# State products and levels of later units in one run on TensorE, outputs and new states laid out by head parity

## The chip, the cores and the metric

One core of one Trainium2 chip runs the whole program in one launch. The metric is the device time in microseconds (us) of one execution; the kernel before has a median of 587.53 us over three runs. Engines are named as in the profile: PE is TensorE (PEld its weight loads), DVE is VectorE, ACT is ScalarE, POOL is GpSimd, SP is SyncE, which issues most transfers.

## The reference

A linear-attention recurrence over 768 steps for 4 batches and 8 heads of width 48 is followed by a two-layer block with `h - tanh(h)` between its matrices, on 3072 tokens:

```python
state = zeros(B, H, D, D)                        # B, H, S, D = 4, 8, 768, 48
for t in range(S):
    cur = einsum('bhd,bhe->bhde', u * k[t], v[t])
    y[t] = einsum('bhd,bhde->bhe', r[t], state + cur)
    state = w * state + einsum('bhd,bhe->bhde', k[t], v[t])
x = y.transpose(0, 2, 1, 3).reshape(B * S, H * D)  # 3072 x 384
h = x @ w_in                                       # 384 -> 2048
out = (h - tanh(h)) @ w_out                        # 2048 -> 384
```

## The kernel before

The recurrence is done in chunks of 64 steps. A *unit* is one chunk (`ch`) of two batches (`z` = 0, 1); there are 24 units, two to a *block* `j` of the dense part, which has 12 blocks. Heads go in pairs: pair `p` = 0 to 3, head parity `i` = 0, 1. Even heads lie in rows 0 to 63, odd heads in rows 64 to 127 (`HEAD[i]`, of which 48 are data); the batch halves of 64 steps lie in `HALF[z]`. TensorE is used in 64x64 tiles for all of this: an operand's row half gives the tile's row, the output's row half its column.

A unit does, in this order:

- `turn`, or for later units `spread_out` and `across`: r and k are turned so that the head width lies across the partitions; scaled by powers of the decay, they become `rT` and `kT`.
- `from_state` (16 products): the state times `rT`, into `y_ps`. It opens the sum over what the unit's outputs will be.
- `levels` (16 products): `kT` times `rT` into `lev`. `V.copy_predicated` (`x.cp`) puts its upper triangle into the tile `at`, whose diagonal ScalarE has written (`diagonal`, L858).
- `outputs`: `v` times `at` is added in `y_ps`; then `to_state`: `kw` times `v` gives what is new in the state, in `kv_ps`.
- `to_xt` and `to_rest` copy `y_ps` on ScalarE, through `given`, to the dense part's operand `xt` and to `rest`. POOL then issues six transfers a block (`fill`, L945), which bring `rest` into the padding rows of `xt`.
- `keep` (L951; for the first two units ScalarE, L954) adds `kv_ps` to the state; `x.decay` (L1002) multiplies it by the decay.

Each product is one call of `put` (L760), and the profile has two matmul instructions for each, so 16 products show as x32. `y_ps` and `kv_ps` are the two halves of the two banks of `yk_ps`. The first dimension of a bank's data is the bank, which is `z` for `y_ps` and `kv_ps` and `i` for `lev`. For units from 2 on (`swap`), the output of parity `i` and batch `z` goes to rows `i ^ z` (`to`), and `given` swaps the odd batch back with two half-row copies.

The first 12 units (*early* ones; `two` is false) have `lev` in banks of their own (`x_banks`), and run `from_state` and `levels` together. The later twelve (`two`) have it in `yk_ps` next to `y_ps`, in the columns where `kv_ps` comes afterwards. For them `from_state` is a step by itself; then a copy of two numbers on ScalarE (`between`, to the tile `seen`, L886) must be done before `levels` may start. `levels` then adds without clearing (`start=not two`).

The dense part goes tile by tile: `h` (L171, TensorE), five passes on ScalarE (L180 to L188), four on VectorE (L195 to L201), then the second matrix, either plainly (`o`, L209) or with seven products for eight (`products`, L260, with sums on POOL at L245 to L249). The first six blocks go through it in passes of 4, 4 and 8 of its 16 column groups (`PASSES`), so that early tiles need only the weights that are converted first: the weights come as 64-bit floats and are converted on VectorE and ScalarE (L139 to L145).

The order on each engine is written out by a planner at build time. Every step is given to it by `add` with an engine, a cost in us, what it comes after, and for TensorE a count of instructions (`steps`). It looks for good due times by random search with a fixed seed, first for a simpler plan, then for the one that is used, which follows the simpler one for the first 90 us of planned time. A change of steps or costs so gives a new order everywhere.

Of the kernel before, what the change touches and what calls it, by code (L numbers as in the profile page):

```python
# [32 lines left out]
PAD = 64  # L33
AHEAD = 2
L = 2
FIRST = 6
# [267 lines left out]
class Plan:  # L304
# [9 lines left out]
    CHUNK, CHUNK_0, ASKED, COMES, FIRST = 256, 192, 55, 3.4, 9.5  # L314
# [233 lines left out]
def near(ctx, tc, r, k, v, w, u, out, shared, moe_w_in, moe_w_out):  # L548
# [3 lines left out]
    V, A, T, G, Q = nc.vector, nc.scalar, nc.tensor, nc.gpsimd, nc.sync  # L552
    d = shared["dims"]
    H, D, NP, NK, B, HEAD = d.H, d.D, d.NP, d.NK, d.B, d.HEAD
# [11 lines left out]
    def fixed(name, shape, dt=F32):  # L566
        return const.tile(shape, dt, name=name, tag=name)
# [9 lines left out]
    HALF = [slice(z * SHORT, (z + 1) * SHORT) for z in range(2)]  # L577
# [2 lines left out]
    rows = fixed("rows", [2 * NP, 2, PAD])  # L580
    V.memset(rows, 1.0)
    same = fixed("same", [128, SHORT])
    seen = fixed("seen", [1, 2])
    V.tensor_tensor(same, ident[:, :SHORT], ident[:, SHORT:], ALU.add)
    by, plus = (work.tile([128, NP, SHORT + 1], F32, name=x, tag=like) for x, like in (("by", "tg"), ("plus", "q")))
    V.memset(by[:, :, 0:1], 0.0)
# [14 lines left out]
    extra = [work.tile([128, 2, NK, PAD], F32, name=f"extra{i}", tag="s") for i in range(L)]  # L601
# [51 lines left out]
    y_ps = yk_ps[:, :, :256].rearrange("e z (p t) -> e z p t", p=NP)  # L653
    kv_ps = yk_ps[:, :, 256 : 256 + NP * D].rearrange("d z (p e) -> d z p e", p=NP)
# [39 lines left out]
    def lay_out(early, across_by):  # L694
# [3 lines left out]
        def add(*args, **more):  # L698
            return plan.add(*args, **more)

        now = [add(e, 1.25 if e == "ACT" else .87, lambda e=e, at=at, x=x: e_of[e].dma_start(out=rows[at : at + NP, :, :D], in_=x.rearrange("(p i) d -> p i d", i=2)), due=-1, data=.05)
               for e, at, x in (("SP", 0, w), ("ACT", NP, u))]
# [3 lines left out]
        now = add("DVE", .45, lambda: V.tensor_scalar(  # L706
            by[:, :, 1:], wcol[:, :, None].to_broadcast([128, NP, SHORT]), W_LOW, W_HIGH, ALU.max, ALU.min), [cols])
        now = add("DVE", .7, lambda: V.tensor_tensor_scan(
            power.rearrange(flat), by.rearrange(flat), plus.rearrange(flat), 0.0, ALU.mult, ALU.add), [now])

        ups = add("ACT", .6, lambda: None, [now])
        now = add("DVE", 1.75, lambda: V.reciprocal(inverse, power), [now])
        inverted = now
        doubled = add("ACT", .6, lambda: A.copy(twice, inverse[:, :, None, 1:].to_broadcast([128, NP, 2, SHORT])), [now])
        now = tabled = add("PE", .7, table, [doubled], steps=8)
# [3 lines left out]
        now = add("POOL", 1.0, bounds, [keeps])  # L719
        now = add("PE", .2, lambda: T.matmul(tab[0:1, 0:1], ok[:, 0, :1], shared["one"], start=True, stop=True), [now, downs])  # L720
        flagged = add("DVE", .15, lambda: V.tensor_scalar(shared["flag"], tab[0:1, 0:1], 128 * NP - 0.5, None, ALU.is_lt), [now])
        bonus = add("SP", .65, lambda: Q.dma_start(
            out=ub.rearrange("p h d -> p (h d)"),
# [17 lines left out]
        for n in range(weights.count):  # L741
# [8 lines left out]
            now = of + ([converted[n - 2]] if n >= 2 else [])  # L750
            for name, cost in (("DVE", .47), ("DVE", .47), ("ACT", .84), ("ACT", .84), ("DVE", .87), ("DVE", .87), ("DVE", .87)):
                now = [add(name, cost, step, now)]
# [6 lines left out]
        def put(*args, **how):  # L759
            T.matmul(*args, skip_group_check=True, **how)  # L760

        units, filled, last_h = [], {}, {}

        def unit(n):
# [5 lines left out]
            ch, half = divmod(n, 2)  # L770
            j, slot = divmod(n, L)
            steps_at = slice(ch * SHORT, (ch + 1) * SHORT)
            t = SimpleNamespace(at=ats[n % 2])
            rt, vt, kw, state = rts[n % (AHEAD + 1)], vts[n % (AHEAD + 1)], kws[n % 2], states[half]
            two = n >= early
# [6 lines left out]
            b1, b2, b3 = (units[n - i] if n >= i else none for i in (1, 2, 3))  # L782
            x = SimpleNamespace(rest=None, rk=None, du=None, own=None)
# [4 lines left out]
            swap = n >= SWAP  # L788
# [67 lines left out]
            def diagonal(hs):  # L856
                for h in hs:
                    A.mul(t.at[:, h % 2, h // 2], same, t.du[:, h : h + 1])  # L858
# [12 lines left out]
            def to(i, z):  # L871


                i = i ^ z if swap else i
                return slice(i * PAD, (i + 1) * PAD)

            def from_state():
                for p in range(NP if ch else 0):
                    for z in range(2):
                        for i in range(2):  # L880
                            put(y_ps[to(i, z), z, p], state[HEAD[i], z, p], t.rT[HEAD[i], p, z],
                                start=p == 0, stop=False)

            def between():

                A.copy(seen, y_ps[:1, :, 0, 0])  # L886

            def levels():
                if not two:
                    from_state()  # L890
                for p in range(NP):
                    for z in range(2):
                        for i in range(2):
                            put(lev[HALF[z], i, p], t.kT[HEAD[i], p, z], t.rT[HEAD[i], p, z], start=not two, stop=True)
# [5 lines left out]
            def outputs():  # L900
                for p in range(NP - direct):
                    for i in range(2):
                        for z in range(2):
                            put(y_ps[to(i, z), z, p], vt[HALF[z], 2 * p + i], t.at[HALF[z], i, p],
                                start=p == 0 and not ch, stop=p == NP - 1)
                for p in range(NK if direct else 0):
                    for i in range(2):
                        for z in range(2):
                            put(y_ps[to(i, z), z, p], extra[slot][HALF[z], i, p], t.at[HALF[z], i, NK],
                                start=False, stop=p == NK - 1)  # L910
                if not direct:
                    to_state()

            def to_state():
                for p in range(NP if more else 0):
                    for i in range(2):
                        for z in range(2):
                            put(kv_ps[i * PAD : (i + 1) * PAD, z, p], kw[HALF[z], 2 * p + i], vt[HALF[z], 2 * p + i, :D],
                                start=p == 0 or not two, stop=True)

            def given(out, y):

                def copy(out, y):
                    A.copy(out, y) if sign > 0 else A.activation(out, y, AF.Copy, scale=sign)  # L924

                if not swap:
                    copy(out, y)
                    return
                copy(out[:, 0], y[:, 0])
                for i in range(2):  # L930
                    copy(out[i * PAD : (i + 1) * PAD, 1], y[to(i, 1), 1])

            def to_xt():
                if slot == 0:
# [3 lines left out]
            def to_rest():  # L938
                if slot == 0:
                    filled[j] = work.tile([128, L, 2, SHORT], F32, name="rest", tag="rest")  # L940
                given(filled[j][:, slot], y_ps[:, :, NK])
# [26 lines left out]
            both = [x.turn, x.turn_k]  # L968
# [8 lines left out]
            if product:  # L977
                now = add("ACT", 1.05, own_k, [x.kT, w_us])
                x.own = add("PE", .7, own_levels, [now, x.rT, b2.out], steps=64)
                x.diag = add("DVE", .64, lambda: V.copy_predicated(t.at, same.bitcast(I32)[:, None, None, :].to_broadcast([128, 2, NP, SHORT]), own_lev), [x.own, b2.out])  # L980
            else:
                x.rk = add(*own_at, own, [x.r, x.k, b2.du, b1.rk if not b1.own else None])
                now = add(*own_at, lambda: V_or_G.tensor_tensor(t.rk, t.rk, ub, ALU.mult), [x.rk, bonus])
                x.du = add("DVE", .47, own_sum, [now, b2.diag])
                now = add("ACT", 1.0, lambda: diagonal(range(0, H // 2)), [x.du, b2.out])
                x.diag = add("ACT", 1.0, lambda: diagonal(range(H // 2, H)), [now])
            begun = []
            if two:
                now = add("PE", .68, from_state, both + [x.rT, b1.xt, b1.rest, b1.add, b2.decay, x.kT], steps=64)
                begun = [add("ACT", .15, between, [now])]  # L990
            x.lev = add("PE", .7 if two else (1.35 if swap else 1.75) if ch else .7, levels,
                        begun + [x.kT, x.rT, b2.out] + ([b2.decay, b1.xt, b1.rest, b1.add] if ch else []), steps=128 if ch and not two else 64)
            x.cp = add("DVE", .64, lambda: V.copy_predicated(t.at, before, lev), [x.lev, b2.out] + ([] if product else [x.diag]))  # L993
            x.out = now = add("PE", .95 if direct else 1.3, outputs,
                              [x.cp, x.diag, x.v, b1.xt, b1.rest, b1.add] + ([x.extra] if direct else [x.kw]), steps=96 if direct else 128)
            if direct:
                now = x.out = add("PE", .6, to_state, [now, x.kw], steps=64)
            x.xt = add("ACT", .96 if swap else .4, to_xt, [now, last_h.get(j - FIRST - 2) if slot == 0 else None])
            if not direct:
                x.rest = add("ACT", .62 if swap else .26, to_rest, [x.xt] + (filled.get((j - 2, "all"), []) if slot == 0 else []))  # L1000
            x.add = add("DVE" if ch else "ACT", .47 if ch else 1.2, keep, [x.out, x.rest, x.xt]) if more else None
            x.decay = x.add if not ch else add(*own_at, lambda: V_or_G.tensor_tensor(state[:, :, :, :D], state[:, :, :, :D], w_all, ALU.mult), [x.add]) if more else None  # L1002
            if direct:
# [95 lines left out]
        for n in range(early):  # L1099
            unit(n)  # L1100
        mixing()
        now, done = 22.0, 0
# [7 lines left out]
        for n in range(early, d.NU):  # L1110
            unit(n)
# [260 lines left out]
def kernel(  # L1372
# [29 lines left out]
    with tc.manual_schedule():  # L1402
        near(tc, r, k, v, w, u, out, shared, moe_w_in, moe_w_out)
# [39 lines left out]
```

## Time and profile before

| what | value |
|---|---|
| median of 3 runs (lowest to highest) | 587.53 us (587.31 to 587.86) |
| span of the profiled execution, first to last instruction | 585.9 us |
| mean granted TensorE clock | 0.999 |
| busy: PE, DVE, ACT, POOL | 570.1, 493.5, 395.6, 206.1 us |
| `h` matmuls, L171 | 281.0 us, 1152 instructions |
| seven products, L260 | 104.1 + 71.5 + 34.8 + 34.7 us |
| small products, L760 on `yk_ps` and `x_ps` | 15 to 16 us for each large group |

The profile shows one execution. For it the span stands, without the launch around it; the runs' median is 1.6 us above it. Busy times are unions of an engine's instructions. Starts of matmuls are measured and their ends are modelled, so the time that a piece of TensorE's work takes is best read from start to start. A row of the timeline merges instructions of one kind that follow each other: start, length, engine, line, operation, output and inputs, shapes, count, and in brackets the idle time before it with what ended it. A row of waits says who waited for whom, for how long in all, and how often.

### The profile page before, as it was taken

To read this page: it belongs to the slowest core of one execution; us is meant where nothing else is said; L and a number is where in the kernel's file an instruction comes from. 1 tells how busy PE (TensorE), PEld (TensorE's weight loads), DVE (VectorE), ACT (ScalarE), POOL (GpSimd) and SP (SyncE) were. 2 spreads that over 40 slices of the span, in tenths; PEclk is the share of its full clock that TensorE was granted. 3 is DMA by queue.
4 is the path that set the end of the run, shared out by engine and by line. 5 is a ranking of instruction groups with operands and counts; after the bars stand their busy time and mean duration, and the time that the engine had idled before them with its cause. 6 is when DMAs were issued, how large, how long until landed. Compare 5 with 4: busy or idle time off the path is not lost.

```text
span 585.9 us, 14391 instructions
## 1 busy us (share of the span) xinstructions
PE 570.1 (97%) x5493; PEld 481.6 (82%) x5493; DVE 493.5 (84%) x817; ACT 395.6 (68%) x893; POOL 206.1 (35%) x366
## 2 busy tenths in 40 slices
PE   8888999999999999999999999999999999999996
PEld 4566677677777699899889898989999899899995
DVE  5799969999999999977988999888877777646665
ACT  2698889979775585555575785775766765665552
POOL 6002212200000245355455465443534446354420
PEclk9999999999999999999999999999999999999999
DMA  6976986743200121232335432531223300100101
GB/s 123 216 146 123 172 201 122 159 107 80 84 0 1 20 49 28 39 56 45 52 55 90 89 57 41 96 45 32 42 43 48 57 3 8 29 8 1 27 2 31
DMA packets 138549, 38.49 MB, mean 66 GB/s; under 512 B 130760, under 2 KB 132904, under 8 KB 138472
## 3 DMA queue, kind: packets, MB, share of 16 engines
q1 hardware_dynamic: 133308, 30.30, 28.4%
q0 software_dynamic: 4992, 6.99, 5.3%
q8 instruction: 45, 0.74, 0.5%
q14 instruction: 32, 0.26, 0.2%
q10 hardware_dynamic: 172, 0.20, 0.1%
HBM read 31.66 MB, written 4.72 MB: 62 GB/s over the span
## 4 chain that ended last, share of the span: by engine, by line
PE 81%; DVE 9%; ACT 4%; issue 2%; DMA 2%; SPq 1%; POOL 0%; DVEq 0%; ACTq 0%; POOLq 0%
PE h L171 38%; PE p L260 27%; PE o L209 7%; PE yk_ps L760 6%; ACT at L858 1%; SPq L798 1%; DMA xt<-rest 1%; DVE g L201 1%; DVE tg L199 1%; PE h L688 1%; DVE g L195 1%; DVE power L144 1%; DVE at L993 1%; DMA first_k<-in_k_dram 1%; DVE tg L197 1%
## 5 line engine op out<-in xcount | busy, mean ns | idle before, releaser
L171 PE MATMUL h<-xt,w_in_sb 128*128 128x256 f32 x1152 | 281.0, 381 | 1.3 <-DVE w_in_sb L145 0.9
L171 PEld LDWEIGHTS h<-xt,w_in_sb 128*128 128x128 f32 x1152 | 213.1, 190 | 32.6 <-PE x_ps L810 1.1
L245 POOL TENSOR_TENSOR sg<-g 128x256 f32<-128x256 f32 x69 | 54.0, 783 | 224.7 <-DVE g L201 213.9
L260 PE MATMUL p<-mixed,sg 128*128 128x192 f32 x426 | 104.1, 326 | 0.0
L197 DVE SCALAR_TENSOR_TENSOR tg<-s,tg 128x512 f32<-128x512 f32 x96 | 70.2, 731 | 30.5 <-ACT tg L184 21.5
L180 ACT ACTIVATE s<-h 128x512 f32<-128x512 f32 x96 | 57.4, 597 | 54.5 <-PE h L171 54.4
L195 DVE TENSOR_TENSOR g<-h,th 128x512 f32<-128x512 f32 x96 | 65.7, 684 | 29.8 <-ACT tg L184 11.1
L182 ACT ACTIVATE th<-h 128x512 f32<-128x512 f32 x96 | 57.3, 597 | 41.7 <-PE h L171 41.7
L184 ACT ACTIVATE tg<-h 128x512 f32<-128x512 f32 x96 | 57.2, 596 | 37.8 <-PE h L171 36.2
L260 PEld LDWEIGHTS p<-mixed,sg 128*128 128x128 f32 x426 | 75.0, 190 | 0.3 <-issue 0.3
L201 DVE COPY_PREDICATED g<-small,tg 128x512 f32<-128x512 int32 x96 | 71.0, 740 | 4.0
L260 PE MATMUL p<-w_out_sb,g 128*128 128x192 f32 x284 | 71.5, 334 | 0.6 <-DVE parts L222 0.6
L209 PE MATMUL o<-w_out_sb,g 128*128 128x384 f32 x192 | 69.8, 490 | 2.1 <-DVE g L201 2.1
L199 DVE SCALAR_TENSOR_TENSOR tg<-q,tg 128x512 f32<-128x512 f32 x96 | 67.7, 705 | 4.1 <-ACT q L186 1.0
L186 ACT ACTIVATE q<-s,m1b 128x512 f32<-128x512 f32 x96 | 69.8, 727 | 0.5
L188 ACT ACTIVATE small<-s,smallb 128x512 f32<-128x512 f32 x96 | 69.6, 725 | 0.3
L260 PEld LDWEIGHTS p<-w_out_sb,g 128*128 128x128 f32 x284 | 52.1, 190 | 8.6 <-DVE parts L222 1.0
L945 POOL DMA_DIRECT2D xt<-rest x66 | 32.4, 498 | 71.4 <-ACT rest L924 71.1
L209 PEld LDWEIGHTS o<-w_out_sb,g 128*128 128x128 f32 x192 | 35.7, 190 | 19.5 <-issue 1.9
L858 ACT ACTIVATE at<-same,du 128x64 f32<-128x64 f32 x184 | 47.9, 340 | 2.0 <-DVE du L854 1.9
L249 POOL TENSOR_TENSOR sg<-sg,g 128x128 f32<-128x128 f32 x69 | 41.4, 600 | 4.9
L247 POOL TENSOR_TENSOR sg<-sg,g 128x128 f32<-128x128 f32 x69 | 40.2, 582 | 4.9
(129 smaller groups left out, 688.8 us busy)
## 6 DMA issues: line engine op xcount, KB each, us to landing
st<-in_moe_w_out_dram SPq DMA_DIRECT2D x8, 768.0 KB, 4.7
rt<-in_r_dram SPq DMA_DIRECT2D x48, 96.0 KB, 3.0
vt<-in_v_dram SPq DMA_DIRECT2D x48, 96.0 KB, 3.1
st<-in_moe_w_in_dram SPq DMA_DIRECT2D x16, 288.0 KB, 5.7
kt<-in_k_dram SPq DMA_DIRECT2D x44, 96.0 KB, 3.2
out_dram<-o POOLq DMA_DIRECT2D x44, 96.0 KB, 2.2
st<-in_moe_w_in_dram POOLq DMA_DIRECT2D x16, 96.0 KB, 5.6
parts<-in_r_dram SPq DMA_DIRECT2D x48, 32.0 KB, 2.1
```

Source lines behind the costliest of these rows:

```text
L171: self.nc.tensor.matmul(t.h2[:, z], self.w_in_sb[:, t.f // 2, kk, z * 128 : (z + 1) * 128], self.xts[t.j][:, kk].rearrange("p b t -> p (b ...
L180: A.activation(out, t.h, AF.Square)
L182: A.activation(out, t.h, AF.Tanh)
L184: A.activation(out, t.h, AF.Tanh, scale=G1)
L186: A.activation(out, t.s, AF.Square, bias=self.m1b)
L188: A.activation(out, t.s, AF.Relu, bias=self.smallb, scale=-1.0)
L195: V.tensor_tensor(t.g, t.h, t.th, ALU.subtract)
L197: V.scalar_tensor_tensor(t.tg, t.s, C4, t.tg, ALU.mult, ALU.mult)
L199: V.scalar_tensor_tensor(t.tg, t.q, K1, t.tg, ALU.add, ALU.mult)
L201: V.copy_predicated(t.g, t.small.bitcast(I32), t.tg)
L209: self.nc.tensor.matmul(self.outs[i], t.g2[:, z, i * C : (i + 1) * C], self.w_out_sb[:, t.f + z, :], start=t.first and z == 0, stop=t.last ...
L260: self.nc.tensor.matmul(ps[bank][:, half * n : (half + 1) * n], a, b, start=t.first and half == 0, stop=t.last, skip_group_check=True)
```

## The change

The outputs `y_ps` are laid out by head parity for the units from 2 on: bank `i` instead of bank `z`; the new states by `z ^ i`. So the state tile's first dimension is `z ^ i` as well. With that, in each step every half (rows 0 to 63 or 64 to 127) of a bank is written from one row half of TensorE only: `HEAD[i]` for `from_state` and `levels`, `HALF[z]` for `outputs` and `to_state`. `from_state` becomes part of `levels` for all units, and the copy `between` and its tile are gone. `given` copies in four half-row pieces instead of one full and two half-row ones. For the first two units (`direct`), `to_xt` comes ahead of `to_state`, which waits for it. Costs given to the planner follow.

```diff
-    seen = fixed("seen", [1, 2])
...
             def from_state():
...
-                            put(y_ps[to(i, z), z, p], state[HEAD[i], z, p], t.rT[HEAD[i], p, z],
+                            put(y_ps[to(i, z), i, p], state[HEAD[i], z ^ i, p], t.rT[HEAD[i], p, z],
                                 start=p == 0, stop=False)
-            def between():
-                A.copy(seen, y_ps[:1, :, 0, 0])
             def levels():
-                if not two:
-                    from_state()
+                from_state()
...
             def outputs():
...
-                            put(y_ps[to(i, z), z, p], vt[HALF[z], 2 * p + i], t.at[HALF[z], i, p],
+                            put(y_ps[to(i, z), i if swap else z, p], vt[HALF[z], 2 * p + i], t.at[HALF[z], i, p],
...
             def to_state():
...
-                            put(kv_ps[i * PAD : (i + 1) * PAD, z, p], kw[HALF[z], 2 * p + i], vt[HALF[z], 2 * p + i, :D],
+                            put(kv_ps[i * PAD : (i + 1) * PAD, z ^ i, p], kw[HALF[z], 2 * p + i], vt[HALF[z], 2 * p + i, :D],
...
             def given(out, y):
...
-                copy(out[:, 0], y[:, 0])
-                for i in range(2):
-                    copy(out[i * PAD : (i + 1) * PAD, 1], y[to(i, 1), 1])
+                for z in range(2):
+                    for i in range(2):
+                        copy(out[i * PAD : (i + 1) * PAD, z], y[to(i, z), i])
...
-            begun = []
-            if two:
-                now = add("PE", .68, from_state, both + [x.rT, b1.xt, b1.rest, b1.add, b2.decay, x.kT], steps=64)
-                begun = [add("ACT", .15, between, [now])]
-            x.lev = add("PE", .7 if two else (1.35 if swap else 1.75) if ch else .7, levels,
-                        begun + [x.kT, x.rT, b2.out] + ([b2.decay, b1.xt, b1.rest, b1.add] if ch else []), steps=128 if ch and not two else 64)
+            x.lev = add("PE", (1.2 if two else 1.35) if ch else .7, levels,
+                        [x.kT, x.rT, b2.out] + ([b2.decay, b1.xt, b1.rest, b1.add] if ch else []), steps=128 if ch else 64)
...
+            x.xt = add("ACT", 1.2 if swap else .4, to_xt, [now, last_h.get(j - FIRST - 2) if slot == 0 else None])
             if direct:
-                now = x.out = add("PE", .6, to_state, [now, x.kw], steps=64)
-            x.xt = add("ACT", .96 if swap else .4, to_xt, [now, last_h.get(j - FIRST - 2) if slot == 0 else None])
+                x.out = add("PE", .6, to_state, [now, x.kw, x.xt], steps=64)
             if not direct:
-                x.rest = add("ACT", .62 if swap else .26, to_rest, [x.xt] + (filled.get((j - 2, "all"), []) if slot == 0 else []))
+                x.rest = add("ACT", .8 if swap else .26, to_rest, [x.xt] + (filled.get((j - 2, "all"), []) if slot == 0 else []))
```

More of the change, by code (lines that the diff above doesn't have):

```diff
@@ L908, in outputs @@
                         for z in range(2):
-                            put(y_ps[to(i, z), z, p], extra[slot][HALF[z], i, p], t.at[HALF[z], i, NK],
+                            put(y_ps[to(i, z), i if swap else z, p], extra[slot][HALF[z], i, p], t.at[HALF[z], i, NK],
                                 start=False, stop=p == NK - 1)
```

## The prediction

> **What bounds the kernel now.** I read the page first: the span, the busy shares and the 40 slices.
>
> ```profile
> span 585.9 us, 14391 instructions
> PE 570.1 (97%) x5493; PEld 481.6 (82%) x5493; DVE 493.5 (84%) x817; ACT 395.6 (68%) x893; POOL 206.1 (35%) x366
> PE   8888999999999999999999999999999999999996
> DVE  5799969999999999977988999888877777646665
> ACT  2698889979775585555575785775766765665552
> PE 81%; DVE 9%; ACT 4%; issue 2%; DMA 2%; SPq 1%; POOL 0%; DVEq 0%; ACTq 0%; POOLq 0%
> ```
>
> TensorE is full in every slice but the first four and the last, and carries 81% of the chain that ended last. So I asked next for the busy time in the two stages that hold the units: the early units (30 to 110 us) and the later ones (285 to 520 us). Columns: window, length, then busy time and instructions of TensorE, its weight loads, VectorE, ScalarE and POOL; then clock and transfers.
>
> ```profile
> 30.00:110.00 80.00, 74.72 (x1453) 56.19 (x1452) 74.48 (x130) 71.03 (x200) 16.43 (x33) 1.00 0.81 152
> 285.00:520.00 235.00, 235.00 (x2547) 210.74 (x2546) 196.35 (x317) 155.74 (x374) 110.49 (x182) 1.00 0.28 48
> ```
>
> The later stage is pure TensorE: 235.00 of 235.00 us busy, VectorE 84%, ScalarE 66%. There a microsecond of TensorE is a microsecond of time. The early stage is another matter: TensorE 93%, VectorE 93%, ScalarE 89%, all three near full, so work added to ScalarE there is not plainly free.
>
> **Term 1: one run in place of two (later units).** The timeline of TensorE shows what a run of small matmuls costs among the dense ones (start, length, instruction, count).
>
> ```profile
> 283.86 1.46 PE L171 MATMUL h<-xt,w_in_sb 128*128 128x256 f32 x6
> 285.25 0.69 PE L760 MATMUL yk_ps<-rT,state 48*64 48x64 f32 x32
> 285.87 1.56 PE L171 MATMUL h<-xt,w_in_sb 128*128 128x256 f32 x6
> 287.36 0.69 PE L760 MATMUL yk_ps<-rT,kT 48*64 48x64 f32 x32
> 287.99 0.59 PE L260 MATMUL p<-w_out_sb,g 128*128 128x192 f32 x2
> ...
> 293.05 0.69 PE L760 MATMUL yk_ps<-at,vt 64*64 64x64 f32 x32
> 293.56 0.63 PE L760 MATMUL yk_ps<-vt,kw 64*64 64x48 f32 x32
> 294.13 0.59 PE L260 MATMUL p<-w_out_sb,g 128*128 128x192 f32 x2
> ...
> 306.56 1.46 PE L171 MATMUL h<-xt,w_in_sb 128*128 128x256 f32 x6
> 307.86 0.49 PE L260 MATMUL p<-w_out_sb,g 128*128 128x192 f32 x2
> ```
>
> Take starts, since ends are modelled. Six dense h matmuls among dense work take 307.86 - 306.56 = 1.30 us. Ahead of the state run they take 285.25 - 283.86 = 1.39 (0.09 more); between the two runs 287.36 - 285.87 = 1.49, so 0.09 for going in again and 0.10 for coming out. The state run itself takes 285.87 - 285.25 = 0.62, the levels run 0.63. Each run thus costs 0.09 + 0.62 + 0.10 = 0.81 to 0.82 us, two of them 1.63. Two sorts of small matmul in one run exist already: outputs and new states take 294.13 - 293.05 = 1.08. The early units run state products and levels together:
>
> ```profile
> 96.17 0.69 PE L760 MATMUL yk_ps<-rT,state 48*64 48x64 f32 x32
> 96.68 0.65 PE L760 MATMUL x_ps<-rT,kT 48*64 48x64 f32 x32
> 97.26 1.56 PE L209 MATMUL o<-w_out_sb,g 128*128 128x384 f32 x4
> ...
> L760 PE MATMUL yk_ps<-rT,state 48*64 48x64 f32 x384 | 8.3, 224 | 0.0
> ```
>
> That is 97.26 - 96.17 = 1.09, with entry and exit 1.28. The saving is 1.63 - 1.28 = 0.35 us a unit. The last row (a group of 285 to 520 us) counts 384 state products, 384/32 = 12 units: **12 x 0.35 = 4.2 us off TensorE**, in the stage where it never idles. The bounds: nothing, if the gap turns into a wait; 12 x 0.36 = 4.3 with the 1.08 row.
>
> A rule of the Trainium skill speaks against this term: "TensorE: Matmul & The Clock Gate", Part 1, states that matmuls never start less than about 25 ns apart. By it a joined run of 64 takes an estimated 1.6 us, 1.79 with entry and exit, and the term becomes 12 x 0.16 = 1.9 us lost, the time 590.3. The trace disagrees: 1.09 us for 64 is 17 ns apart, so the sum goes by the row.
>
> **Term 2: the handshake on ScalarE goes.**
>
> ```profile
> L886 ACT COPY seen<-yk_ps x12: 133/133/150, 286.8 to 508.6; 1x2 f32<-1x2 f32 x12
>   PE yk_ps L760: 1.8, 4
>   DVE tg L197: 1.7, 1
> ```
>
> Twelve copies of 0.13 us and their waits leave ScalarE. Nobody who waited for them was TensorE (one VectorE instruction, 1.7 us), and the dense work between the two runs hid them. Zero. What is late next is the copy of the levels by predicate on VectorE, which TensorE need not meet soon: 287.99 to 293.05 is 5 us of other work.
>
> **Term 3: four copies of 64 rows for three (units 2 to 23).** `given` issues one more instruction for xt and one more for rest. Groups of ScalarE from 30 to 110 us:
>
> ```profile
> L924 ACT ACTIVATE xt<-yk_ps 64x192 f32<-64x192 f32 x10 | 3.3, 325 | 0.1
> L924 ACT ACTIVATE rest<-yk_ps 64x64 f32<-64x64 f32 x10 | 2.2, 219 | 0.1
> L924 ACT COPY xt<-yk_ps 128x192 f32<-128x192 f32 x5 | 1.6, 323 | 1.2 <-PE yk_ps L760 1.2
> ```
>
> Half the rows cost as much as all (325 ns against 323), so the added pair is 0.325 + 0.219 = 0.54 us a unit: 5.4 us on ScalarE for the ten early units and 12 x (0.54 - 0.13) = 4.9 for the later ones. The later stage has 235 - 155.7 = 79 us of idle ScalarE, and a unit comes only every 20 us there: zero. If that cover were gone it would cost 4.9.
>
> In the early stage ScalarE idles 80 - 71.0 = 9.0 us; 5.4 fits, leaving 3.6. But the pair lies on each unit's own circle: outputs, xt, rest, addition to the state, next unit's levels. How much reaches TensorE? The waits from 30 to 120 us name that path (total, times, longest):
>
> ```profile
> PEld yk_ps L760 <- DVE state L951: 2.3, 4, 0.7
> PE yk_ps L760 <- ACT st L142: 1.1, 1, 1.1
> PE h L171 <- DMA xt<-rest: 0.3, 1, 0.3
> PE yk_ps L760 <- DVE state L951: 0.3, 1, 0.3
> ```
>
> Ten units with three copies each of 0.325 and 0.219 are 16 us of copying, and behind it stand 0.3 (matmuls) to 2.6 us (with their weight loads) of TensorE waiting. The same share of 5.4 is 0.1 to 0.9. The bounds are 0, because idle ScalarE covers it, and 5.4, because every copy may be met. I take the upper end of the nearest rows: **0.9 us lost**. The transfers that fill the padding from POOL's queue start 0.5 us later per pair of units; their longest named wait is the 0.3 above, inside the bound.
>
> **Term 4: units 0 and 1, the new wait.** Their new states now wait for the xt copy.
>
> ```profile
> 22.80 0.53 PE L760 MATMUL yk_ps<-at,extra 64*64 64x64 f32 x24
> 23.26 0.66 PE L810 MATMUL x_ps<-ident,rt 128*128 128x128 f32 x4
> 23.84 0.68 PE L760 MATMUL yk_ps<-vt,kw 64*64 64x48 f32 x32
> 24.62 0.49 ACT L924 ACTIVATE xt<-yk_ps 128x384 f32<-128x384 f32 x1 [2.36 <-PE yk_ps L760]
> 25.69 1.04 ACT L954 ACTIVATE state<-yk_ps,power 128x96 f32<-128x96 f32 x4
> 26.78 0.56 PEld L760 LDWEIGHTS yk_ps<-rT,state 48*64 48x64 f32 x32 [0.78 <-ACT state L954]
> 32.00 0.24 PE L760 MATMUL yk_ps<-at,vt 64*64 64x64 f32 x1 [1.11 <-ACT st L142]
> ```
>
> Outputs end at 23.33; ScalarE idles, so the copy runs from about 23.5 to 24.0, and the new states go at 24.1 instead of 23.84: 0.3 later, with the next transposes and filler queued behind them. But ScalarE then has the copy behind it, and the state at L954 can start at 24.9 instead of 25.69. Bounds: 0.3 lost, 0.8 gained. Neither survives: TensorE stands at 32.00 for the conversion of weights (ACT st). Zero. The other relabelled banks and halves change addresses, not counts: zero.
>
> **Sum.** -4.2 + 0 + 0.9 + 0 = -3.3 us on the profiled 585.9, so a span of 582.6. The median of the runs is 587.53, 1.6 us above the span; with the same 1.6 the time is **584.2 us**.
>
> **The rivals.**
> - *ScalarE becomes the bound of the early stage* (ends slower). Place: 30 to 110 us. With 5.4 us more it is at 76.4 of 80. If each added pair is met on the unit's circle, TensorE loses all 5.4: 587.5 - 4.2 + 5.4 = 588.7; if each of the ten units then also meets the longest wait above, 0.7, it is 595.7. It outweighs the saving from a loss of 4.2. For it: ScalarE's 89% and VectorE's 93% in that window. Against it: only 0.3 to 2.6 us of waiting in that place now. Chance 12%, 10 of it beyond 588.7. *A part of it*, a loss of 2 to 4.2, gives 585.3 to 587.5: 14%.
> - *VectorE takes over later.* The joined run saves TensorE time only if g and the others keep pace. VectorE is at 196 of 235 us, 85% afterwards. If half the gain becomes waits: 585.4 to 587.5. 6%; against it, TensorE waits for nobody in this stage today.
> - *Two row tiles in one bank hold each other up.* After the change each outputs run writes a bank from both row tiles; before, the state run did. If a pair went one after the other, 32 matmuls would take 0.51 us longer, 12 x 0.51 = 6.1 later and up to 5.1 early: 590.3 to 595.4. The state run of before already does it, at 0.62 us, no longer than the levels. 2%.
>  The Trainium skill, "TensorEngine Tiling (Array Packing)", Gotcha 1, says that different row tiles cannot access one bank simultaneously. By that rule this rival holds; the state run's trace disagrees as far as time goes.
> - *More comes back.* The written-out order is searched anew, with earlier xt copies in units 0 and 1; TensorE idles 5.3 us between 30 and 110. If 1.5 or more of that goes: under 582.7. 6%.
>
> **How the numbers follow.** My forecast (582.7 to 585.3) has 60%. A difference of 0.2% is 1.2 us, about what a measurement of this kernel tells from none. Faster than 586.3: 60 + 6 (more) + 7 (half the part) + 3 (half of VectorE's) = 76%. Within: 7 + 3 + 2 = 12%. Slower: 10 + 2 = 12%. The range of 8 in 10 runs from 582.3 to 588.0; it leaves out most of the 6% below and the 10 + 2% above.
>
> **What would show it.** Right: twelve runs of 64 small matmuls, 1.08 to 1.10 us from first start to the next dense start, no `seen` row, TensorE full from 285 us on; four rows of 64x192 and of 64x64 for each unit after the first two; TensorE at the same places of its work at most 1 us later at 120 us. Wrong: ScalarE at 9 tenths and over from 30 to 110 us with TensorE waiting for the state addition or xt there; or outputs runs whose 32 matmuls take over 0.6 us; or gaps on TensorE after 285 us that name VectorE.

## The result, and the profile after

The changed kernel takes 590.5 us (median; 589.75 to 591.83) where the kernel before takes 587.69 beside it: a ratio of 1.0051, with a 95% interval of 1.0036 to 1.0066. It is slower by about half a percent. I had forecast 584.2 us and a range up to 588.0. Of the runs below one, of the kernel before with another seed, took 3357.31 us; it is left out of that kernel's median.

The page of the kernel after (span, busy shares, slices, chain):

```profile
span 590.1 us, 14406 instructions
PE 569.5 (97%) x5501; PEld 482.9 (82%) x5501; DVE 491.6 (83%) x817; ACT 407.5 (69%) x925; POOL 205.4 (35%) x366
PE   7797999999999999999999999999999999999995
ACT  2698899978777575655576777686766757575552
PE 77%; issue 6%; DVE 6%; DMA 4%; POOL 2%; ACT 2%; SPq 2%; DVEq 0%; POOLq 0%; ACTq 0%
```

TensorE is 0.6 us less busy than before, and the span is 4.2 us longer: in sum the time is in gaps. PE's share of the chain fell from 81% to 77%. The two stages again (window, length, busy time of PE, PEld, DVE, ACT, POOL):

```profile
30.00:110.00 80.00, 73.63 (x1346) 53.91 (x1349) 73.15 (x126) 71.79 (x208) 16.06 (x32) 1.00 0.79 145
285.00:520.00 235.00, 235.00 (x2569) 214.38 (x2569) 197.72 (x326) 164.86 (x394) 113.45 (x188) 1.00 0.29 49
```

Late, TensorE is as full as it was. Early, it has 1346 instructions in the window where it had 1453, and idles 6.4 us instead of 5.3. The joined run does what was said of it. From TensorE's timeline after:

```profile
305.44 0.69 PE L759 MATMUL yk_ps<-rT,state 48*64 48x64 f32 x32
305.95 0.65 PE L759 MATMUL yk_ps<-rT,kT 48*64 48x64 f32 x32
306.53 0.59 PE L260 MATMUL p<-w_out_sb,g 128*128 128x192 f32 x2
...
308.05 0.69 PE L759 MATMUL yk_ps<-at,vt 64*64 64x64 f32 x32
308.56 0.63 PE L759 MATMUL yk_ps<-vt,kw 64*64 64x48 f32 x32
```

306.53 - 305.44 = 1.09 us for 64, as in the early units; and outputs that write one bank from both row tiles take 308.56 - 308.05 = 0.51, as they did when each bank was written from one.

To see on which side the time went, I cut each trace at the first of the seven-for-eight products (L260), which come when the passes over early tiles end. The rows give the shortest, median and longest duration, then the first and last start. Before:

```profile
L260 PE MATMUL p<-w_out_sb,g x284: 326/326/430, 203.9 to 577.2; 128*128 128x192 f32 x142
```

After:

```profile
L260 PE MATMUL p<-w_out_sb,g x284: 326/326/431, 209.1 to 579.7; 128*128 128x192 f32 x142
```

Up to the cut, 5.2 us are lost, and really 6.5: the next rows count the h matmuls ahead of it, 330 before and 324 after, so six of them (1.3 us) moved behind the cut. (The plain products `o`, L209, ahead of it are 192 in both.)

```profile
0.00:203.80 203.80, 79.41 (x330) 1.00 0.55 111
```

```profile
0.00:209.00 209.00, 78.68 (x324) 0.99 0.56 109
```

From the cut to the last product it is 373.3 us before and 370.6 after, 369.3 without those six: **4.0 us gained late, 6.5 lost early**. Ahead of the cut TensorE is also busier, 195.6 us against 193.1. Of this 2.7 us are fill matmuls on `ident` (44 in place of 36, at L688 before and L687 after), which the planner puts where it expects TensorE to wait; whether they hold anything up was not tried. The profiled execution also ends 1.7 us later after its last product (590.1 - 579.7 = 10.4 against 8.7); it took 591.83 us and is the longest of the four. The same order with three copies, below, has 586.6 - 577.9 = 8.7 there, so that piece most likely belongs to this execution and not to the change.

### The profile page after: what moved, and what is told of

It reads as the page before. It is cut to its first block, busy times and chain, and to the rows that moved or that the text cites. A ratio compares the mean times of both kernels' runs of the same rounds, so it can differ in the third digit from the quotient of the medians.

```text
span 590.1 us, 14406 instructions
## 1 busy us (share of the span) xinstructions
PE 569.5 (97%) x5501; PEld 482.9 (82%) x5501; DVE 491.6 (83%) x817; ACT 407.5 (69%) x925; POOL 205.4 (35%) x366
## 4 chain that ended last, share of the span: by engine, by line
PE 77%; issue 6%; DVE 6%; DMA 4%; POOL 2%; ACT 2%; SPq 2%; DVEq 0%; POOLq 0%; ACTq 0%
PE h L171 38%; PE p L260 26%; PE o L209 7%; PE yk_ps L759 5%; DMA xt<-rest 2%; DMA st<-in_moe_w_in_dram 1%; POOL xt L939 1%; SPq L797 1%; DVE g L201 1%; DVE power L144 1%; DVE tg L199 1%; DVE g L195 1%; DVE tg L197 1%; PE p L209 0%; PE h L687 0%
## 5 line engine op out<-in xcount | busy, mean ns | idle before, releaser
L260 PE MATMUL p<-mixed,sg 128*128 128x192 f32 x426 | 104.1, 326 | 0.2 <-issue 0.2
L260 PEld LDWEIGHTS p<-mixed,sg 128*128 128x128 f32 x426 | 75.1, 190 | 0.4 <-POOL sg L245 0.4
L209 PE MATMUL o<-w_out_sb,g 128*128 128x384 f32 x192 | 70.0, 491 | 2.2 <-DVE g L201 2.0
L260 PE MATMUL p<-w_out_sb,g 128*128 128x192 f32 x284 | 70.7, 331 | 0.0
L260 PEld LDWEIGHTS p<-w_out_sb,g 128*128 128x128 f32 x284 | 52.7, 190 | 7.6 <-DVE parts L222 0.2
L209 PEld LDWEIGHTS o<-w_out_sb,g 128*128 128x128 f32 x192 | 35.6, 190 | 20.1 <-DVE g L201 1.7
```

The source lines that it names most:

```text
L209: self.nc.tensor.matmul(self.outs[i], t.g2[:, z, i * C : (i + 1) * C], self.w_out_sb[:, t.f + z, :], start=t.first and z == 0, stop=t.last ...
L260: self.nc.tensor.matmul(ps[bank][:, half * n : (half + 1) * n], a, b, start=t.first and half == 0, stop=t.last, skip_group_check=True)
```

## The experiments

Four things changed at once in the early stage: a fourth copy per xt and rest; the order in which everything is issued, since other steps and costs make the planner's random search end elsewhere; the wait in units 0 and 1; and the banks of outputs and states. The theories: A, the copies cost the early stage its time; B, the new order does.

**Four copies in the kernel before.** Costs and steps as they were, so the order is that of before; only `given` differs:

```diff
-                copy(out[:, 0], y[:, 0])
-                for i in range(2):
-                    copy(out[i * PAD : (i + 1) * PAD, 1], y[to(i, 1), 1])
+                for z in range(2):
+                    for i in range(2):
+                        copy(out[i * PAD : (i + 1) * PAD, z], y[to(i, z), z])
```

> The kernel before with its own written-out order and layout, each xt and rest copy of units 2 to 23 issued in four half-row pieces (one more each, 0.54 us a unit on ScalarE). Theory A (the added copies on ScalarE cost the early stage its 7 us): 5 to 7 us slower than before, 592.5 to 594.5. Theory B (the new written-out order costs it): at most the 0.9 us of my third term slower, 587.7 to 588.6, and TensorE at the same place of its dense work at 120 us within 1 us.

590.42 us against 587.92, ratio 1.0044 (1.0030 to 1.0058): 2.5 us, between the two expectations. All of it is early:

```profile
L260 PE MATMUL p<-w_out_sb,g x284: 326/326/430, 206.6 to 579.9; 128*128 128x192 f32 x142
```

The cut is 2.7 us later, and from there it takes 373.3 us, as before: four copies cost nothing in the later stage. The copies cost more than my 0.9, and less than the 6.5 that is lost.

**Three copies in the changed kernel.** The reverse, in the changed kernel's order: `given` has the three copies of before. This leaves out the regrouping of odd heads and batches, so the second matrix gets other rows; the amount of work is the same.

> The changed kernel with its own order, the copies issued as before the change: bank 0 whole, bank 1 in two half-row pieces (the regrouping of odd heads and batches is left out, so the second matrix gets other rows). Theory A: the early stage gets its 7 us back, 583 to 585.5. Theory B: 0 to 1.5 us faster than the changed kernel, 589 to 590.5.

588.27 us, ratio to before 0.9999 (0.9988 to 1.0010); 2.2 us faster than with four, again between the two expectations. So the copies cost 2.2 to 2.5 us in either order, and without them the change, with 4 us gained late, is still only level with before. Something else costs another 4.

**The due times of before for the changed kernel.** The simpler plan keeps the separate state step, the hand-over and the old costs:

```diff
+            old, begun = across_by == "PE", []
+            if old and two:
+                now = add("PE", .68, lambda: None, both + [x.rT, b1.xt, b1.rest, b1.add, b2.decay, x.kT], steps=64)
+                begun = [add("ACT", .15, lambda: None, [now])]
...
+                x.xt.key, x.out.key = x.out.key, x.xt.key
```

(The last line gives xt and new states of units 0 and 1 the due times of the same steps of before. The levels' cost and count and the copies' costs, left out here, are the old ones too.)

> The changed kernel in full, but the planner's simpler plan is made from the steps and costs of before, and the copies keep their old costs, so that the due times of the first 90 us are those of before. Theory A: early loss as after, late gain as after, 589 to 591. Theory B: the early stage as before and the late gain of 4.2 kept, 583.5 to 585.

593.19 us, ratio 1.0090 (1.0076 to 1.0104): worse, against both theories. The edit didn't do what I meant. The due times of the first 90 us were those of before, but the order was not: the list scheduler, with other steps among the ready ones, again issued other work first: on ScalarE from the place on that has the diagonals at 28.37 us before, on VectorE from that of `tg` at 34.39. It shows only that the changed kernel, in another order and at these costs, can take 2.7 us more.

**Another seed for the kernel before.** Same steps, same costs, another order: `Random(6)` in place of `Random(5)`.

> The kernel before with another seed (6 for 5) in the planner's random search: same steps, another order. Theory A (orders that the search finds are alike): 587.0 to 588.5. Theory B (they differ by microseconds): over 1 us away from 587.7 on either side, with the difference made in the first 120 us.

592.75 us, ratio 1.0082 (1.0064 to 1.0100). So an order alone is worth about 5 us, in a kernel in which nothing else is changed. I had expected the difference in the first 120 us. It is spread wider: the cut is at 206.0, with 324 h matmuls ahead of it, so of 5.4 us of span 2.1 + 1.3 = 3.4 are lost ahead of the cut and 2.0 behind it. The scatter made it necessary to hold the order fixed.

**The change in the order of before.** The planner gets the steps and costs of before; at the place of the levels step the state products run too, and at the state step's and the hand-over's places nothing. Early units stay as they were, and the two states are regrouped once between the stages:

```diff
             def across_r():
+                if n < early + 2:
+                    odd = state[PAD:]
+                    kept = work.tile([128, NP, PAD], F32, name="rk", tag="rk")[PAD:]
+                    G.tensor_copy(kept, odd[:, 0])
+                    G.tensor_copy(odd[:, 0], odd[:, 1])
+                    G.tensor_copy(odd[:, 1], kept)
...
             def levels():
-                if not two:
-                    from_state()
+                from_state()
...
-                now = add("PE", .68, from_state, both + [x.rT, b1.xt, b1.rest, b1.add, b2.decay, x.kT], steps=64)
-                begun = [add("ACT", .15, between, [now])]
+                now = add("PE", .68, lambda: None, both + [x.rT, b1.xt, b1.rest, b1.add, b2.decay, x.kT], steps=64)
+                begun = [add("ACT", .15, lambda: None, [now])]
```

(With `i if two else z` for the bank of `y_ps`, `z ^ i if two else z` for the state's, and the four copies for later units alone.)

> The kernel before with its own order, costs and early units; in the later units alone state products run inside the levels' place, outputs lie by parity and are copied in four pieces; the two states are regrouped once on POOL between the stages (three small copies each). Theory B (late gain real, loss from the new order and the early copies): 587.8 - 4.2, 583.2 to 584.2, twelve runs of 1.09 us. Theory C (the late gain is given back late, by ScalarE's four copies or VectorE): 586 or more, with gaps on TensorE after 285 us.

583.81 us, ratio **0.9931** (0.9917 to 0.9944): 4.0 us faster than before. The cut stands where it stood, and the later part takes 369.4 us in place of 373.3:

```profile
L260 PE MATMUL p<-w_out_sb,g x284: 326/326/430, 204.0 to 573.4; 128*128 128x192 f32 x142
```

Theory C (the gain is given back late) falls: four copies and all, nothing is given back. The six copies on POOL are hidden.

**The same, with four copies in the early units too.** This is the change in the order of before, but without the wait in units 0 and 1 and with the banks of before in the early units.

> The same as the kernel with kept order and only the later units changed, with four copies in the early units too: the whole change but for units 0 and 1, in the order of before. Theory B: the early copies cost what they cost in the kernel before, 2.5 us: 585.5 to 586.7, so faster than before. Theory A (the added copies alone make the changed kernel slow): 590 or more.

586.51 us, ratio 0.9973 (0.9963 to 0.9983): faster than before, and 2.7 slower than with three early copies. The difference is all ahead of the cut:

```profile
L260 PE MATMUL p<-w_out_sb,g x284: 326/326/430, 206.5 to 575.8; 128*128 128x192 f32 x142
```

The waits of both from 30 to 120 us (total, times, longest) say where. Three early copies:

```profile
PEld yk_ps L760 <- DVE state L961: 2.3, 4, 0.7
PE yk_ps L760 <- DVE state L961: 0.3, 1, 0.3
DVE state L961 <- ACT rest L929: 0.3, 1, 0.3
```

Four:

```profile
PEld yk_ps L760 <- DVE state L956: 5.0, 6, 1.5
PE yk_ps L760 <- DVE state L956: 1.7, 3, 1.1
DVE state L956 <- ACT rest L929: 1.1, 3, 0.5
```

It is the circle that I had named: rest on ScalarE, state on VectorE, next unit's products on TensorE. TensorE's weight loads wait 5.0 - 2.3 = 2.7 us more for the state, which is what the cut and the time show.

**Is the changed kernel's order worse by nature?** Seeds 6, 7 and 8 for both kernels. D: an order is a draw. E: the change leads the search to worse orders.

> The changed kernel with seed 6 in the planner's search. Theory D (which order the search happens on weighs several us, and the order of before is a good draw): within 3 us of the kernel before with seed 6 less 1.8, 588.5 to 594.5. Theory E (the change's steps and costs make all orders worse): at least 593, slower than the kernel before with that seed.

> The kernel before with seed 7. Theory D: again slower than with its own seed, 589 to 594. If seed 6 was the odd one: 587 to 588.5.

> The changed kernel with seed 7. With the order held fixed the change was worth 1.3 us (586.5 against 587.85). Theory D (an order is a draw, and no worse under the change): within 3.5 us of the kernel before with seed 7 less 1.3, 591 to 598. Theory E (the change's steps and costs lead the search to worse orders): about 3 us above the kernel before with seed 7, as with seeds 5 and 6: 598 to 600.

> The kernel before with seed 8. Theory D: over 1 us slower than with seed 5, 589 to 597, which makes seed 5 the best of four. Otherwise 586 to 589.

> The changed kernel with seed 8. Theory D: anywhere within 3.5 us of the kernel before with seed 8 less 1.3. Theory E: 2 to 4 us above it.

| seed | before, us | changed, us | difference |
|---|---|---|---|
| 5 (as given) | 587.7 | 590.5 | +2.8 |
| 6 | 592.75 | 596.21 | +3.5 |
| 7 | 595.77 | 590.60 | -5.2 |
| 8 | 594.07 | 590.59 | -3.5 |
| mean | 592.6 | 592.0 | -0.6 |

After seed 6 it looked like E: the difference was about +3 a second time, and 596.21 lies above D's 588.5 to 594.5. Seeds 7 and 8 turned the sign, seed 7 by a little more than D had allowed. E falls; of D, the sign is free as it says, but its width of 3 to 3.5 us was too narrow in two of three draws. With four draws that scatter by several us, the mean of -0.6 can't be told from -1.3, which the change is worth in a fixed order, nor from nothing. But one thing stands out: of four orders for the kernel before, that of seed 5 is the best, by 5 us. Any edit that changes the planner's steps gives this draw away.

What a worse order looks like, in one early unit: rows of the timeline from the outputs' new states (which end at 42.98 and 44.34, where TensorE's next run starts) to the next unit's state products and the first h matmuls of the block whose `rest` is copied here. Before:

```profile
42.42 0.63 PE L760 MATMUL yk_ps<-vt,kw 64*64 64x48 f32 x32
...
43.66 0.98 ACT L924 ACTIVATE xt<-yk_ps 128x192 f32<-128x192 f32 x3
44.65 1.06 ACT L858 ACTIVATE at<-same,du 128x64 f32<-128x64 f32 x4
45.62 0.68 ACT L924 ACTIVATE rest<-yk_ps 128x64 f32<-128x64 f32 x3
...
46.07 1.53 PE L209 MATMUL o<-w_out_sb,g 128*128 128x384 f32 x4 [1.56 <-DVE g L201]
46.35 2.91 POOL L945 DMA_DIRECT2D xt<-rest  x6 [29.68 <-ACT rest L924]
46.41 0.55 DVE L951 TENSOR_TENSOR state<-yk_ps,state 128x384 f32<-128x384 f32 x1
...
47.52 0.69 PE L760 MATMUL yk_ps<-rT,state 48*64 48x64 f32 x32
...
52.11 2.75 PE L171 MATMUL h<-xt,w_in_sb 128*128 128x256 f32 x12
```

The changed kernel:

```profile
43.77 0.63 PE L759 MATMUL yk_ps<-vt,kw 64*64 64x48 f32 x32
...
44.74 1.07 ACT L857 ACTIVATE at<-same,du 128x64 f32<-128x64 f32 x4 [1.00 <-DVE du L853]
45.71 1.32 ACT L918 ACTIVATE xt<-yk_ps 64x192 f32<-64x192 f32 x4
...
47.52 0.92 ACT L918 ACTIVATE rest<-yk_ps 64x64 f32<-64x64 f32 x4
...
48.49 2.90 POOL L939 DMA_DIRECT2D xt<-rest  x6 [31.72 <-ACT rest L918]
48.56 1.53 PE L209 MATMUL o<-w_out_sb,g 128*128 128x384 f32 x4 [0.98 <-DVE g L201]
48.75 0.56 DVE L945 TENSOR_TENSOR state<-yk_ps,state 128x384 f32<-128x384 f32 x1
...
50.01 0.69 PE L759 MATMUL yk_ps<-rT,state 48*64 48x64 f32 x32
...
56.76 2.98 PE L171 MATMUL h<-xt,w_in_sb 128*128 128x256 f32 x12 [1.99 <-DMA xt<-rest]
```

Before, xt starts 0.7 us behind that end, and the state is ready (46.41 + 0.55) 4.0 us behind it. After, a row of diagonals stands ahead of xt and waits 1.00 us for `du`, so xt starts 1.4 us behind, and the state is ready 5.0 behind. Of this 1.0 us the fourth copies are 0.6 (1.32 - 0.98 and 0.92 - 0.68); the rest is place in the queues. The next state products, 4.5 and 5.7 us behind, are not held by the state here: in both kernels they start 1.45 us behind the start of four plain products, which had waited for `g`.

What TensorE does meet is the padding. POOL issues the six transfers right behind `rest`; before, they have landed when the h matmuls come at 52.11, and after, TensorE waits 1.99 us for them and starts at 56.76. That is 4.65 us later than before. With four copies in the order of before (the kernel before with four copies, and the last of the kept-order runs) these h matmuls start at 52.13 and 52.20, so the copies alone don't make this loss. The transfers issued from 46 to 57 us (count, size, median us to landing), before and then after:

```profile
xt<-rest POOLq DMA_DIRECT2D x6, 16.0 KB, 2.6
```

```profile
st<-in_moe_w_in_dram SPq DMA_DIRECT2D x2, 288.0 KB, 5.2
xt<-rest POOLq DMA_DIRECT2D x6, 16.0 KB, 5.9
```

In the new order two loads of weights of 288 KB, which the kernel before issues at other times, start at 49.31, in the midst of these transfers. That they slow them is argued, and was not tried alone. From 30 to 120 us, TensorE's matmuls wait for these transfers 2.0, 1.7, 1.3 and 1.4 us in the changed kernel with seeds 5 to 8, and 0.3 us and three times nothing in the kernel before; so this piece came with all four orders that the search found for the change. With three copies in the changed kernel's order it is 0.4, but a wait of 1.4 us for weights follows at the same place.

## Why the prediction was wrong

- *Term 1, the joined run:* right. Forecast 4.2 us; measured 4.0 in a fixed order (587.85 to 583.81), and 4.0 behind the cut in the changed kernel. The 25 ns rule of the Trainium skill ("TensorE: Matmul & The Clock Gate", Part 1) would have had it lose; 64 matmuls again start within 1.09 us, 17 ns apart.
- *Term 2, the handshake, and the later copies:* right as far as seen, nothing. With four copies in the kernel before, the later part is 373.3 us, unchanged; the handshake was not taken out alone.
- *Term 3, the early copies:* the mechanism was right, the size was not. I took 0.9 us, by giving the added copies the share of waiting that the present ones had; they cost 2.2 to 2.7. The step that failed is the proportion: here the waiting grew faster than the copying. The four waits of before were at most 0.7 us; half a microsecond more for each unit made six waits of up to 1.5. That this is so because the circle's slack is used up from some point on fits these waits and was not tried with other lengths. The bound of 5.4 held. The padding transfers, which I had put inside it by their longest wait of 0.3 us, cost TensorE 2.0 us in the changed kernel's order.
- *Term 4, units 0 and 1:* open. The wait was not tried alone, and the kept-order runs leave it out. In the changed kernel the next unit's state products start at 40.21, where before has 39.39, and TensorE waits for nothing between 24.41 and there; the four-copy kernel, whose first state products came 1.4 us late, starts them at 39.39 too. So 0.8 us in all were lost by then, by this wait or by the new order; they lie in the 4.0 below.
- *The order:* the larger step that failed. In the rivals I let the new search only bring something back (6%), and gave it no term. What the changed kernel takes above the run with four copies in the order of before is 590.5 - 586.5 = 4.0 us, the largest early item, and its sign was open. This 4.0 is a remainder: it holds the new order and what that run leaves out, the wait in units 0 and 1 and the early banks. With seeds that draw 587.7 to 595.8 us for the kernel before, a term of some us to the slower side for leaving a good draw belonged into the sum's range, and the range to 588.0 was far too narrow for it.
- *Two row tiles in one bank* (the Trainium skill, "TensorEngine Tiling (Array Packing)", Gotcha 1): no sign of it in time, 0.51 us for the outputs run in both kernels. *VectorE late:* no; TensorE stays at 235.00 of 235.00.

The sum as measured: -4.0 (joined runs) + 2.7 (early copies) + 4.0 (order and the rest) = +2.7 us, against +2.8 measured. It closes because the last term is what was left over.

What stays open: how the 4.0 divides. By the h matmuls at 56.76 us that much is lost (4.65 us against before), 2.0 of it in the wait for the padding. The places ahead of that were not taken apart, nor was the share of TensorE's clock (last section).

## What to carry to other kernels

Where a planner or a search writes the order, first run the unchanged kernel with a few other seeds: the scatter (here 8 us, or 1.4%) is the ruler for any edit that changes its steps or costs, and the order that is in place may be the best of many. Judge the edit itself in the old order, by giving the planner the old steps and letting the new work run at their places: here the edit, but for units 0 and 1 and the early banks, went from a loss of 2.8 us to a gain of 1.3, and with the early units left alone (583.81 us) to one of 4.0, which beats both kernels. And an added half microsecond on a circle that is nearly tight can cost more than its share of the waiting seen so far.

## What the runs showed of the hardware

TensorE's clock dipped in the first 40 us of many runs; in the order of before that cost nothing. Windows of the four-copy kernel (columns as above; the third number from the end is the granted clock):

```profile
20.00:25.00 5.00, 2.71 (x90) 2.31 (x90) 3.52 (x7) 2.09 (x3) 0.00 (x0) 1.00 1.08 177
25.00:30.00 5.00, 5.00 (x72) 2.57 (x71) 4.60 (x8) 4.80 (x15) 0.00 (x0) 0.66 1.06 322
```

TensorE was busy 2.71 of 5 us; then the clock stood at 0.66 on average for 5 us. In the profile of before, in the same order, TensorE had 4.09 of 5 us there and no dip:

```profile
20.00:25.00 5.00, 4.09 (x92) 2.80 (x93) 3.68 (x8) 2.10 (x3) 0.00 (x0) 1.00 1.03 171
25.00:30.00 5.00, 4.88 (x79) 3.31 (x78) 4.35 (x8) 4.91 (x16) 0.00 (x0) 1.00 1.05 323
```

Both start the state products at 39.39 us, and in both TensorE waits 0.22 us right before for VectorE's `rT`, so TensorE did not set the pace there. The run with three early copies in the order of before has the same dip (0.66) and its cut at 204.0, as before; so the 2.7 us of the four copies are not the dip's. Nor does the time follow the clock in that order: in the last of the kept-order kernels, runs with a mean granted clock of 0.995 took 586.28 and 586.77 us, and runs with 1.000 took 585.93 and 586.58.

In orders that the search found for the changed kernel it does. With seed 8 the run at 0.989 took 594.43 us, and the two at 1.000 took 589.17 and 589.30; with seed 7 it is 592.88 at 0.988 and 587.62 at 0.998; with three copies and seed 5 it is 589.32 at 0.994 and 586.25 at 0.998. (The changed kernel's own four runs don't say: 591.21 at 0.992 and 589.75 at 0.997, but 591.83 and 589.78 both at 0.996.) There TensorE was full behind the gap: in the profile after it has 15.00 of 15.00 us from 25 to 40, and the clock stands at 0.66 in the first five of them, which would be 1.7 us of work if all of it counted (an estimate, 0.34 x 5). Whether the dip makes these runs long, or something late makes both the dip and the length, no run here tells apart; a part of the order's 4.0 us may be the clock's.

A page of the Trainium skill ("TensorE: Matmul & The Clock Gate", Part 1) lets the clock fall to half after an idle window of about 3.4 us. These windows agree in kind only: in the four-copy kernel the clock stood at 0.50 from 25.5 to 28.5 us, but the gap on TensorE ahead of it was 2.29 us.
